# Opening of the first MLP: float32 squares and first copies on ScalarE, weights converted three steps after their load, one slice and one batch a step sooner

## The chip, the cores and the metric

The kernel runs on one core of a Trainium2 chip. The metric is the device time of one execution in microseconds (us), taken over several runs; lower is better. Times below are on the clock of one profiled execution, from the start of its span.

## What is computed

Attention over eight batches and eight heads with 32 learned packing queries, then two feed-forward blocks. Everything is float32; precision is kept by splitting each operand into a rounded high part and the rest, and multiplying three times (high x high, low x high, high x low).

```python
def sm_attn(qq, kk, vv):
    s = scale * np.matmul(qq, kk.transpose(0, 1, 3, 2))
    s = s - np.max(s, axis=-1, keepdims=True)
    a = np.exp(s)
    a = a / (np.sum(a, axis=-1, keepdims=True) + 1e-09)
    return np.matmul(a, vv)
p_packed = sm_attn(p, k, v)            # 8 x 8 x 32 x 64
out = sm_attn(q, p_packed, p_packed)   # 8 x 8 x 576 x 64
# x = out as 4608 tokens x 512
h = np.maximum(x @ w_in, 0.0)          # 512 x 2048
x = h * h @ w_out                      # 2048 x 512
# then a second MLP (512 x 1024 x 512) with SoLU and layer norm
```

## The kernel before, in words

The weights arrive as 64-bit floats. `Decode` (L105 to L133) loads one piece as pairs of 32-bit words (`raw`) and makes float32 of it (`dw`): ScalarE scales the high word (L122), VectorE shifts and merges bits (L123, L127, L129). Then ScalarE rounds the high part (`ws` for w_in, L271; `woh` for w_out, L320) and GpSimd takes the rest (L55).

The output projection of the attention is folded into the first weight matrix. `Unit.product` (L278) multiplies a unit, 256 rows by 256 columns of w_in, with the packed values `L` of four batches into PSUM (`pw`); ScalarE and VectorE copy it to `pws` as high and low part (L293, L294); and the sync queue (SP), which issues all transfers in program order, stores it at the head of the next step. Batch 0's columns of slices 0 and 1 go straight to `slot` in SBUF; all others go to `pw_d` in device memory and are read back by `load_slot` as needed. A slice is 256 of the 2048 hidden columns; there are eight. It is made from two units and serves two blocks of 128 columns, so four steps of a batch.

Then come the steps of the first MLP, listed in `steps`: each is (batch, half of its 576 tokens, block `fc` of 128 hidden columns). In step i, `h1` (L400) multiplies the attention weights of its batch (`ah`, `al`: high and low part) by the slot, and ScalarE takes the relu (`rg`, L413), GpSimd its float32 square (L414), ScalarE the rounded square (L415), VectorE the difference (L55). Four steps later `ymm` (L419) multiplies by w_out into the four PSUM tiles `Y`. Batches 0 and 1 go first and in turns: steps 0 to 3 use slice 0 of batch 0, 4 to 7 its slice 1, 8 to 15 both slices of batch 1, 16 and 17 slice 2 of batch 0, 18 and 19 its slice 3. Because Y is summed over a few blocks at a time there, it is copied out (L439 on ScalarE, L441 on VectorE) and later added to (L437). The first copies come at steps 5, 7, 15 and 19.

`clock` counts the steps of the outer loop (from L811): ten for the attention of the first packing, then T0 = 10 is step 0. `at_step` (L458) puts a load at a step; `unit_at` (L469) and `wout_at` (L481) put the three parts of a conversion k, k and k+1 steps behind it. `s2_jobs` (L329) lists the parts of one score slice of a batch: matmuls `s` against the packed keys `slc`, transposes, softmax, and the split into ah and al. PSUM tiles of `pw`, `h` and `s` share four banks.

Matmuls on TensorE, the sync queue and a few copies keep program order (`keep_in_program_order`, the calls through `pin`). All other instructions are put in order per engine by the tile framework, which simulates a timeline. At run time every engine runs its list in order: an instruction that waits holds up what is behind it.

Of the kernel before, what the change touches and what calls it, by code (L numbers as in the profile page):

```python
# [15 lines left out]
AF = mybir.ActivationFunctionType  # L16
ALU = mybir.AluOpType
# [18 lines left out]
def build(tc, qT, kT, vP, pT, w_in, w_out, w_in2, w_out2, g_ln, out):  # L36
    nc = tc.nc

    TURN = {n: cycle(x) for n, x in {"ETC": "VVA", "LNA": "AAAV"}.items()}
    V, A, G, PE, SP = nc.vector, nc.scalar, nc.gpsimd, nc.tensor, nc.sync  # L40


# [2 lines left out]
    def mm(*a, **k):  # L45
        pin(PE.matmul(*a, **k))  # L46

    def flip(own, *a):
        (pin if own else lambda x: x)(PE.transpose(*a))
# [94 lines left out]
    class Pack:  # L144
# [71 lines left out]
        def transp(self, n):  # L216
            t = self.pl.tile([P, KC * P], F32, tag="eT", name="eT", bufs=2) if self.own else t25("2", "eT")
            self.eT[n] = t.rearrange("p (k c) -> p k c", k=KC)
            for a, b in ((0, 3), (3, KC)):
                pt = bank("pt")[:, :(b - a) * P]  # L220
                for c in range(a, b):
                    flip(self.own, pt[:, (c - a) * P:(c - a + 1) * P], self.e1[n % 2][:, c * P:(c + 1) * P], ident)
                if next(TURN["ETC"]) == "A":
                    A.copy(t[:, a * P:b * P], pt)
# [33 lines left out]
    T0 = 10  # L258
    ring, clock = [0], [0]
# [140 lines left out]
    def h1(n):  # L400
        b, half, fc = n
        c = slice(half * HF, (half + 1) * HF)
        pb = bank("h1")
        w = slot[b, fc // 2][:, :, fc % 2]
        i = 0
        for g in range(2):
            ah, al = at[b, g]
            for l, x in ((0, ah), (1, ah), (0, al)):
                mm(pb[:, :HF], w[:, g, l], x[:, c], start=(i == 0), stop=(i == 5))
                i += 1  # L410
        rg, g2 = t25("1", "rg"), t25("2", "ghl", F32R)
        r, gg, gh, gl = rg[:, :HF], rg[:, HF:S], g2[:, :HF], g2[:, HF:S]
        A.activation(r, pb[:, :HF], AF.Relu)  # L413
        G.tensor_tensor(out=gg, in0=r, in1=r, op=ALU.mult)  # L414
        A.activation(gh, r, AF.Square)  # L415
        split_lo(V, gl, gg, gh)
        gt[n] = (gh, gl)

    def ymm(n):  # L419
        b, half, fc = n  # L420
        gh, gl = gt.pop(n)
        wh, wl = wo[fc]
        firsts = cuts.get(b, whole)
        for oc in range(4):
            o = slice(oc * P, (oc + 1) * P)
            for i, (w, x) in enumerate(((wh, gh), (wl, gh), (wh, gl))):
                mm(Y[oc], w[:, o], x, start=(fc in firsts and i == 0), stop=(fc + 1 in firsts and i == 2))
        if fc + 1 in firsts:
            c0 = b * S + half * HF
            new = (b, half) not in yp  # L430
            if new:
                yp[b, half] = ypp.tile([P, 4 * HF], F32, name=f"yp{half}") if b == 1 else sums()
            t = yp[b, half]
            for oc in range(4):
                o = t[:, oc * HF:(oc + 1) * HF]
                if not new:
                    V.tensor_tensor(out=o, in0=Y[oc], in1=o, op=ALU.add)  # L437
                elif oc % 2 == 0:
                    A.copy(o, Y[oc])  # L439
                else:  # L440
                    V.tensor_copy(o, Y[oc])  # L441
            if fc == 15:
                later.append(lambda: dma(y_d[:, :, c0:c0 + HF], t.rearrange("p (o c) -> p o c", o=4)))
# [25 lines left out]
    def unit_at(i, bg, s, g, pl, bufs):  # L469
        d = {}  # L470

        def begin():
            d["u"] = Unit(bg, s, g, pl(), bufs)
            queue.append(d["u"])

        at_step("first" if i == -5 else i, begin)
        k = 3 if i < -5 else 4
        for j in (k, k, k + 1):
            at_step(i + j, lambda: d["u"].d.step())

    def wout_at(i, fc):  # L481
        d = {}
        at_step("first" if i == -5 else i, lambda: d.setdefault("u", wout_unit(fc, win)))
        if i == -5:
            i = -4 + fc
        k = 3 if i < 0 else 4
        for j in (k, k, k + 1):
            at_step(i + j, lambda: d["u"].step())

    for b in range(2, B):  # L490
# [9 lines left out]
        for s in range(8):  # L500
            i = 16 + 2 * s + 3
            if b == 2:
                i = (17, 19, 21, 23, 25, 31, 33, 35)[s]
            if b == 4:
                i = max(i, 9 + 4 * s)
            at_step(base + i, lambda b=b, s=s: load_slot(b, s))
    for s, (i, k) in enumerate(((None, 4), (None, 6), (12, 13), (15, 16), (25, 26), (29, 30), (39, 40), (43, 44))):
        if i:
            at_step(i, lambda s=s: load_slot(0, s))
        at_step(k, lambda s=s: load_slot(1, s))  # L510
# [109 lines left out]
    for n in range(8):  # L620
        i = P1 + 1 + PS * n
# [109 lines left out]
    def h2(m):  # L731
# [15 lines left out]
        for i, h in enumerate(t):  # L747
# [16 lines left out]
            G.tensor_tensor(out=rstd, in0=rstd, in1=mhalf, op=ALU.pow)  # L764
            if next(TURN["LNA"]) == "V":
                V.tensor_scalar(out=h, in0=h, scalar1=mv[:, 0:1], scalar2=rstd, op0=ALU.subtract, op1=ALU.mult)
# [27 lines left out]
    def products():  # L794
        while queue and queue[0].ready():
            queue.pop(0).product()

    ps1 = {}
    early = {}
# [11 lines left out]
    for t in range(max(max(j for j in jobs if j != "first"), T0 + N + LAG - 1) + 2):  # L811
        i = t - T0
        clock[0] = t
        for fn in later:
            fn()
        later.clear()
        for n in ((0,), (1,), (2,), (3,), (4, 5), (6, 7))[t] if t < 6 else ():
            K0.load_v(n)
        if t + 3 < H:
            K0.load_k(t + 3)  # L820
        if t + 1 < H:
            K0.scores(t + 1)
        if t == 3:
            load_q(0)
        if t == 5:
            load_q(1)
            for j in jobs.pop("first"):
                j()
        if t == H:
            ps0_st.close()  # L830
            ps1["p"], ps1["st"] = pool("ps1", space=PSUM)
            Y += [ps1["p"].tile([P, HF], F32, name=f"Y{o}") for o in range(4)]
        if 0 <= t - 1 < H:
            K0.transp(t - 1)
        if t + 1 < H:
            K0.soft(t + 1)
        if 0 <= t - 2 < H:
            K0.packed(t - 2)
        if t in (4, 6, 8, 9):
            K0.pairs(t // 2 - 2 if t < 9 else 3)  # L840
        if t <= 9:
            products()
        if t == 6:
            for j in s2_jobs(0, 0, q0[0]):
                j()
        if t == 9:
            early[0] = s2_jobs(0, 1, q0[1], 2)
            for j in early[0][:9]:
                j()
            open_b()  # L850
            early[1] = s2_jobs(1, 0), s2_jobs(1, 1)
            for x in early[1]:
                x.pop(0)()
            early[1] = early[1][0] + early[1][1]
        if 0 <= i < N:
            h1(steps[i])
        for j in jobs.get(t, ()):
            j()
        products()
        if i == 0:  # L860
            for j in early[0][9:]:
                j()
        if 2 <= i < 8:
            for j in early[1][3 * i - 6:3 * i - 3]:
                j()
        if 0 <= i - LAG < N:
            ymm(steps[i - LAG])
# [121 lines left out]
```

## Time and profile before

| | us |
|---|---|
| runs of before | 1253.58, 1257.25, 1254.42 |
| median | 1254.42 |
| profiled execution, its own time | 1250.78 |
| its span in the profile | 1249.0 |
| TensorE busy in the span | 1159.8 |
| VectorE, ScalarE, GpSimd busy | 874.9, 639.3, 610.7 |

In the rows below PE is TensorE's matmuls, PEld its weight loads, DVE VectorE, ACT ScalarE, POOL GpSimd, SP the sync engine. L46 is line 46 of the kernel; as a helper issues matmuls, they are told apart by their tiles (out<-in, the numbers of the buffers left out). The time in brackets behind a row is how long the engine was idle ahead of it and what ended that. A matmul of 288 columns shows as 0.44 us or 0.30 us according to the clock that was granted.

### The profile page before, as it was taken

The numbers are of one execution on the slowest core, as the hardware profiler recorded it, in microseconds if no ns is written. First come the engines' busy times: TensorE is split into PE (matmuls) and PEld (weight loads), VectorE is DVE, ScalarE is ACT, GpSimd is POOL, SyncE is SP. The second block draws the span as 40 slices with busy tenths as digits, with TensorE's granted clock in tenths as the row PEclk, the third lists the DMA queues.
The fourth block names the chain that finished last, engine by engine and source line by source line (L and its number), as shares of the span: only waits on it lengthen the run. The fifth ranks groups of instructions, "written<-read, shape, count | busy, mean of one in ns | idle before, by whom it ended". The sixth has DMA issues, their size and how long they took to land.

```text
span 1249.0 us, 23478 instructions
## 1 busy us (share of the span) xinstructions
PE 1159.8 (93%) x8556; PEld 1064.5 (85%) x8556; DVE 874.9 (70%) x1722; ACT 639.3 (51%) x1413; POOL 610.7 (49%) x652
## 2 busy tenths in 40 slices
PE   6777699999999989999999999999999899998998
PEld 3456698898999878999999999998888788887888
DVE  4777588755436776575657733449898889989886
ACT  3444455444445554454555544346665556665554
POOL 1055355533324454443434433126886877886853
PEclk9768799999999998999999999999999999999999
DMA  9755777775144889556373482351112111111101
GB/s 329 228 169 141 230 218 231 259 253 189 59 171 148 250 249 305 161 177 250 139 281 134 157 334 104 124 168 35 34 40 64 34 39 63 35 39 42 56 27 43
DMA packets 97540, 187.66 MB, mean 150 GB/s; under 512 B 13968, under 2 KB 41616, under 8 KB 97424
## 3 DMA queue, kind: packets, MB, share of 16 engines
q1 hardware_dynamic: 97424, 186.16, 45.3%
q8 instruction: 67, 1.10, 0.4%
q14 instruction: 49, 0.40, 0.1%
HBM read 119.02 MB, written 66.06 MB: 148 GB/s over the span
## 4 chain that ended last, share of the span: by engine, by line
PE 60%; DVE 13%; POOL 10%; issue 6%; DMA 6%; ACT 4%; SPq 1%; ACTq 0%; DVEq 0%; POOLq 0%
PE Y L46 29%; PE h L46 13%; PE o L712 6%; PE h L712 5%; POOL y L682 3%; POOL cl L892 3%; PE s L46 3%; DMA yf<-y_d 2%; PE pw L46 2%; POOL rstd L764 1%; DVE dw L127 1%; POOL yf L675 1%; DMA raw<-w_out 1%; DVE dw L129 1%; DMA raw<-w_in 1%
## 5 line engine op out<-in xcount | busy, mean ns | idle before, releaser
L46 PE MATMUL Y<-ghl,woh 128*128 128x288 f32 x2048 | 469.4, 305 | 6.2 <-DVE yp L437 4.6
L46 PEld LDWEIGHTS Y<-ghl,woh 128*128 128x128 f32 x2048 | 349.9, 192 | 22.1 <-issue 8.5
L414 POOL TENSOR_TENSOR rg<-rg 128x288 f32<-128x288 f32 x256 | 188.3, 736 | 355.6 <-ACT rg L413 349.2
L46 PE MATMUL Y<-ghl,wol 128*128 128x288 f32 x1024 | 306.7, 300 | 0.0
L55 DVE TENSOR_TENSOR ghl<-rg,ghl 128x288 fp32r<-128x288 f32 x256 | 144.3, 567 | 201.8 <-ACT ghl L415 190.7
L46 PE MATMUL h<-ah,slot 128*128 128x288 f32 x1024 | 219.4, 303 | 24.3 <-ACT ah L388 9.2
L415 ACT ACTIVATE ghl<-rg 128x288 fp32r<-128x288 f32 x256 | 113.8, 445 | 189.3 <-PE Y L46 187.3
L712 PE MATMUL o<-wx,ch 128*128 128x256 f32 x1008 | 192.8, 288 | 8.7 <-ACT ch L891 4.7
L46 PEld LDWEIGHTS Y<-ghl,wol 128*128 128x128 f32 x1024 | 197.0, 192 | 0.0
L46 PEld LDWEIGHTS h<-ah,slot 128*128 128x128 f32 x1024 | 170.8, 195 | 27.6 <-issue 16.1
L712 PEld LDWEIGHTS o<-wx,ch 128*128 128x128 f32 x1008 | 162.5, 194 | 19.8 <-DVE ys L729 7.1
L46 PE MATMUL h<-al,slot 128*128 128x288 f32 x512 | 154.2, 301 | 0.9 <-POOL al L55 0.9
L712 PE MATMUL o<-wx,cl 128*128 128x256 f32 x504 | 143.3, 288 | 3.8 <-POOL cl L892 3.8
L892 POOL TENSOR_TENSOR cl<-raw,ch 128x512 fp32r<-128x512 f32 x84 | 120.3, 1439 | 41.1 <-ACT ch L891 40.9
L413 ACT ACTIVATE rg<-h 128x288 f32<-128x288 f32 x256 | 104.2, 407 | 55.3 <-PE h L46 46.9
L682 POOL TENSOR_TENSOR y<-yf,y 128x256 fp32r<-128x256 f32 x111 | 97.2, 887 | 31.1 <-ACT y L679 29.0
L712 PEld LDWEIGHTS o<-wx,cl 128*128 128x128 f32 x504 | 96.9, 194 | 6.6 <-POOL cl L892 5.3
L46 PEld LDWEIGHTS h<-al,slot 128*128 128x128 f32 x512 | 99.4, 194 | 1.2 <-POOL al L55 1.2
L891 ACT CAST ch<-raw 128x512 fp32r<-128x512 f32 x126 | 76.0, 620 | 39.2 <-DVE raw L897 25.2
L712 PE MATMUL h<-wi,y 128*128 128x512 f32 x312 | 84.2, 404 | 2.0 <-DVE hs L729 1.9
L679 ACT CAST y<-yf 128x256 fp32r<-128x256 f32 x120 | 47.0, 406 | 58.2 <-DVE yf L675 28.5
L55 POOL TENSOR_TENSOR ws<-dw,ws 128x512 fp32r<-128x512 f32 x32 | 41.9, 1312 | 70.4 <-ACT ws L271 70.4
(148 smaller groups left out, 1873.5 us busy)
## 6 DMA issues: line engine op xcount, KB each, us to landing
pw_d<-pws SPq DMA_DIRECT2D x124, 256.0 KB, 4.5
slot<-pw_d SPq DMA_DIRECT2D x62, 512.0 KB, 6.0
raw<-w_in SPq DMA_DIRECT2D x40, 512.0 KB, 6.2
raw<-w_out SPq DMA_DIRECT2D x24, 512.0 KB, 6.4
kf<-kT SPq DMA_DIRECT2D x32, 288.0 KB, 5.1
yf<-y_d SPq DMA_DIRECT2D x36, 256.0 KB, 3.0
out<-ys SPq DMA_DIRECT2D x72, 128.0 KB, 1.7
vf<-vP SPq DMA_DIRECT2D x16, 512.0 KB, 7.0
```

The lines of the kernel that those rows point to most:

```text
L46: pin(PE.matmul(*a, **k))
L55: eng.tensor_tensor(out=lo, in0=x, in1=f(hi), op=ALU.subtract)
L127: V.scalar_tensor_tensor(out=x, in0=self.hi, scalar=0x80000000, in1=x, op0=ALU.bitwise_and, op1=ALU.bitwise_or)
L129: V.scalar_tensor_tensor(out=x, in0=self.lo, scalar=29, in1=x, op0=ALU.logical_shift_right, op1=ALU.bitwise_or)
L413: A.activation(r, pb[:, :HF], AF.Relu)
L414: G.tensor_tensor(out=gg, in0=r, in1=r, op=ALU.mult)
L415: A.activation(gh, r, AF.Square)
L679: i = A.copy(c[n][0], x)
L682: (V if YS[cnt[1] % len(YS)] == 'V' else G).tensor_tensor(out=c[n][1], in0=x, in1=f(c[n][0]), op=ALU.subtract)
L712: PE.matmul(bk, x, w[:, y], start=(i == 0), stop=(i == 3 * nk - 1))
L891: A.copy(c[n][0], x)
L892: eng.tensor_tensor(out=c[n][1], in0=x, in1=f(c[n][0]), op=ALU.subtract)
```

## The change

In the first 20 steps the float32 square moves from GpSimd to ScalarE, and ScalarE makes all four first copies of Y instead of two. Units and pieces of w_out that are loaded before step 14 are converted three steps behind their load instead of four; the units of slice 1, loaded ahead of step 0, are then finished before step 0, and their products come two steps sooner. At the last step before step 0 the score matmuls of batch 0's second half go ahead of the product of the unit that is ready. Slice 2 is read back one step sooner for batches 0 and 1. The score jobs of batch 1 run four a step in steps 1 to 5 instead of three a step in steps 2 to 7. Copies of the transposed weights (`ETC`) alternate between VectorE and ScalarE, instead of two and one.

```diff
--- before.py
+++ after.py
@@ -36,7 +36,7 @@
 def build(tc, qT, kT, vP, pT, w_in, w_out, w_in2, w_out2, g_ln, out):
     nc = tc.nc
 
-    TURN = {n: cycle(x) for n, x in {"ETC": "VVA", "LNA": "AAAV"}.items()}
+    TURN = {n: cycle(x) for n, x in {"ETC": "VA", "LNA": "AAAV"}.items()}
     V, A, G, PE, SP = nc.vector, nc.scalar, nc.gpsimd, nc.tensor, nc.sync
 
 
@@ -411,7 +411,10 @@
         rg, g2 = t25("1", "rg"), t25("2", "ghl", F32R)
         r, gg, gh, gl = rg[:, :HF], rg[:, HF:S], g2[:, :HF], g2[:, HF:S]
         A.activation(r, pb[:, :HF], AF.Relu)
-        G.tensor_tensor(out=gg, in0=r, in1=r, op=ALU.mult)
+        if clock[0] < T0 + 20:
+            A.activation(gg, r, AF.Square)
+        else:
+            G.tensor_tensor(out=gg, in0=r, in1=r, op=ALU.mult)
         A.activation(gh, r, AF.Square)
         split_lo(V, gl, gg, gh)
         gt[n] = (gh, gl)
@@ -435,7 +438,7 @@
                 o = t[:, oc * HF:(oc + 1) * HF]
                 if not new:
                     V.tensor_tensor(out=o, in0=Y[oc], in1=o, op=ALU.add)
-                elif oc % 2 == 0:
+                elif oc % 2 == 0 or clock[0] < T0 + 20:
                     A.copy(o, Y[oc])
                 else:
                     V.tensor_copy(o, Y[oc])
@@ -474,7 +477,7 @@
             queue.append(d["u"])
 
         at_step("first" if i == -5 else i, begin)
-        k = 3 if i < -5 else 4
+        k = 3 if i < 14 else 4
         for j in (k, k, k + 1):
             at_step(i + j, lambda: d["u"].d.step())
 
@@ -483,7 +486,7 @@
         at_step("first" if i == -5 else i, lambda: d.setdefault("u", wout_unit(fc, win)))
         if i == -5:
             i = -4 + fc
-        k = 3 if i < 0 else 4
+        k = 3 if i < 14 else 4
         for j in (k, k, k + 1):
             at_step(i + j, lambda: d["u"].step())
 
@@ -504,7 +507,7 @@
             if b == 4:
                 i = max(i, 9 + 4 * s)
             at_step(base + i, lambda b=b, s=s: load_slot(b, s))
-    for s, (i, k) in enumerate(((None, 4), (None, 6), (12, 13), (15, 16), (25, 26), (29, 30), (39, 40), (43, 44))):
+    for s, (i, k) in enumerate(((None, 4), (None, 6), (11, 12), (15, 16), (25, 26), (29, 30), (39, 40), (43, 44))):
         if i:
             at_step(i, lambda s=s: load_slot(0, s))
         at_step(k, lambda s=s: load_slot(1, s))
@@ -838,14 +841,17 @@
             K0.packed(t - 2)
         if t in (4, 6, 8, 9):
             K0.pairs(t // 2 - 2 if t < 9 else 3)
-        if t <= 9:
+        if t < 9:
             products()
         if t == 6:
             for j in s2_jobs(0, 0, q0[0]):
                 j()
         if t == 9:
             early[0] = s2_jobs(0, 1, q0[1], 2)
-            for j in early[0][:9]:
+            for j in early[0][:2]:
+                j()
+            products()
+            for j in early[0][2:9]:
                 j()
             open_b()
             early[1] = s2_jobs(1, 0), s2_jobs(1, 1)
@@ -860,8 +866,8 @@
         if i == 0:
             for j in early[0][9:]:
                 j()
-        if 2 <= i < 8:
-            for j in early[1][3 * i - 6:3 * i - 3]:
+        if 1 <= i < 6:
+            for j in early[1][4 * i - 4:4 * i]:
                 j()
         if 0 <= i - LAG < N:
             ymm(steps[i - LAG])
```

How the instructions move, at three places. First TensorE around the products of slice 1 (`pw`, 12 matmuls a unit; `h` is a step, `s` a score slice of batch 1). Before, from step 1 on:

```order
L46 MATMUL h_790<-ah,slot 128x288 x2
L46 MATMUL h_790<-al,slot 128x288
L46 MATMUL h_790<-ah,slot 128x288 x2
L46 MATMUL h_790<-al,slot 128x288
L46 MATMUL h_809<-ah,slot 128x288 x2
L46 MATMUL h_809<-al,slot 128x288
L46 MATMUL h_809<-ah,slot 128x288 x2
L46 MATMUL h_809<-al,slot 128x288
L46 MATMUL pw<-ws,L 128x256 x24
L46 MATMUL s_869<-qf,slc 64x288 x2
L46 MATMUL s_870<-qf,slc 64x288 x2
```

Now, from the product of slice 0 that stood ahead of the scores of step 0:

```order
L46 MATMUL pw<-ws,L 128x256 x12
L46 MATMUL h_758<-ah,slot 128x288 x2
L46 MATMUL h_758<-al,slot 128x288
L46 MATMUL h_758<-ah,slot 128x288 x2
L46 MATMUL h_758<-al,slot 128x288
L46 MATMUL pw<-ws,L 128x256 x24
L46 MATMUL h_843<-ah,slot 128x288 x2
L46 MATMUL h_843<-al,slot 128x288
L46 MATMUL h_843<-ah,slot 128x288 x2
L46 MATMUL h_843<-al,slot 128x288
L46 MATMUL s_866<-qf,slc 64x288 x2
L46 MATMUL s_867<-qf,slc 64x288 x2
```

The 24 matmuls of slice 1 stand behind step 0 (h_758) instead of behind step 2 (h_809), and the scores of batch 1 behind step 1 instead of step 2.

Second, the sync queue after the first stores of slice 0 (`slot<-pws` and `pw_d<-pws` store a unit, `raw` loads weights, `slot<-pw_d` reads a slice back):

```order
-L52 DMA raw<-w_out 128x1024
-L52 DMA raw<-w_in 128x2x512
-L52 DMA raw<-w_out 128x1024
-L52 DMA slot<-pws 32x512 x4
-L52 DMA pw_d<-pws 32x4x512 x3
-L52 DMA slot<-pws 32x512 x4
-L52 DMA pw_d<-pws 32x4x512 x3
+L52 DMA slot<-pws 32x512 x4
+L52 DMA pw_d<-pws 32x4x512 x3
+L52 DMA slot<-pws 32x512 x4
+L52 DMA pw_d<-pws 32x4x512 x3
+L52 DMA raw<-w_out 128x1024
+L52 DMA raw<-w_in 128x2x512
+L52 DMA raw<-w_out 128x1024
```

The stores of slice 1's two units are now ahead of three weight loads that stood before them.

Third, ScalarE around the copies of slice 3's two products (`pws`), before:

```order
L320 CAST woh4_1323<-dw_1289 128x512
L122 ACTIVATE dw_1327<-raw_1138 128x512
L293 CAST pws_1346<-pw_1332 128x2x2x128
L293 CAST pws_1346<-pw_1333 128x2x2x128
L415 ACTIVATE ghl_1375<-rg_1374 128x288
L413 ACTIVATE rg_1428<-h1_1421 128x288
L439 COPY yp0_1453<-Y0_600 128x288
L439 COPY yp0_1453<-Y2_602 128x288
L320 CAST woh5_1382<-dw_1327 128x512
L293 CAST pws_1400<-pw_1386 128x2x2x128
L293 CAST pws_1400<-pw_1387 128x2x2x128
```

And now:

```order
L320 CAST woh4_1296<-dw_1258 128x512
L122 ACTIVATE dw_1300<-raw_1166 128x512
L293 CAST pws_1321<-pw_1307 128x2x2x128
L293 CAST pws_1321<-pw_1308 128x2x2x128
L418 ACTIVATE ghl_1350<-rg_1349 128x288
L413 ACTIVATE rg_1401<-h1_1394 128x288
L415 ACTIVATE rg_1401<-rg_1401 128x288
L320 CAST woh5_1355<-dw_1300 128x512
L293 CAST pws_1373<-pw_1359 128x2x2x128
L293 CAST pws_1373<-pw_1360 128x2x2x128
```

The second product's copies (pws_1373) stand ahead of the copies of Y; the relu between is that of step 14 (rg_1401) instead of step 15, and the new float32 square follows it (L415, in place on rg).

## Rows read from the trace of the kernel before

**Rows 1.** Head of the profile page.
```profile
span 1249.0 us, 23478 instructions
```
**Rows 2.** Stretches: length; busy (count) of PE, PEld, DVE, ACT, POOL; clock; DMA share; GB/s.
```profile
60.00:80.00 20.00, 12.59 (x56) 9.00 (x55) 17.81 (x28) 10.42 (x22) 10.92 (x10) 0.50 0.51 147
80.00:102.00 22.00, 14.53 (x83) 13.19 (x84) 15.53 (x25) 10.29 (x23) 12.20 (x13) 0.81 0.53 161
102.00:148.00 46.00, 34.67 (x225) 32.02 (x225) 31.37 (x50) 20.04 (x44) 19.18 (x19) 0.83 0.73 200
148.00:260.00 112.00, 107.35 (x786) 101.65 (x787) 83.34 (x149) 57.37 (x131) 52.45 (x58) 0.96 0.72 234
```
**Rows 3.** Waits of TensorE from 50 to 260 us: total us, times, longest.
```profile
PE h L46 <- ACT ah L388: 9.2, 2, 5.1
PE h L46 <- DMA slot<-pws: 6.2, 2, 4.3
PE h L46 <- DMA slot<-pw_d: 6.1, 1, 6.1
...
PE h L46 <- DVE pws L294: 2.8, 1, 2.8
```
**Rows 4.** Timeline of TensorE: start, us, what, times, idle before.
```profile
59.58 0.85 PE L46 MATMUL h<-ah,slot 128*128 128x288 f32 x2 [4.04 <-ACT ah L388]
...
68.47 1.22 PE L46 MATMUL pw<-ws,L 64*128 64x256 f32 x8 [0.56 <-POOL ws L55]
...
81.47 0.82 PE L46 MATMUL h<-ah,slot 128*128 128x288 f32 x2 [4.33 <-DMA slot<-pws]
...
86.52 1.19 PE L46 MATMUL s<-qf,slc 128*64 128x288 f32 x8
...
102.00 0.44 PE L46 MATMUL Y<-ghl,woh 128*128 128x288 f32 x1
```
**Rows 5.** Groups by line, 59 to 148 us: busy us, mean ns, idle before.
```profile
L414 POOL TENSOR_TENSOR rg<-rg 128x288 f32<-128x288 f32 x18 | 14.8, 822 | 46.4 <-ACT rg L413 46.4
...
L122 ACT ACTIVATE dw<-raw 128x512 f32<-128x512 f32 x14 | 9.2, 664 | 1.2 <-POOL wol L55 1.0 <-POOL ws L55 0.2
...
L415 ACT ACTIVATE ghl<-rg 128x288 fp32r<-128x288 f32 x18 | 8.0, 444 | 10.6 <-PE Y L46 10.3
...
L439 ACT COPY ys<-Y 128x288 f32<-128x288 f32 x4 | 1.6, 396 | 1.6 <-PE Y L46 1.6
```
**Rows 6.** Timeline of ScalarE, 114 to 138 us.
```profile
114.38 0.65 ACT L122 ACTIVATE dw<-raw 128x512 f32<-128x512 f32 x1
...
123.84 0.62 ACT L271 CAST ws<-dw 128x512 fp32r<-128x512 f32 x1 [2.63 <-DVE dw L129]
...
128.29 0.62 ACT L320 CAST woh<-dw 128x512 fp32r<-128x512 f32 x1 [2.64 <-DVE dw L129]
...
129.38 1.06 ACT L293 CAST pws<-pw 128x512 fp32r<-128x512 f32 x2
...
136.08 1.07 ACT L293 CAST pws<-pw 128x512 fp32r<-128x512 f32 x2
```
**Rows 7.** Timeline of the sync queue, 71 to 80 us.
```profile
71.56 0.34 SPq L52 DMA_DIRECT2D raw<-w_out  x1
72.00 2.42 SPq L52 DMA_DIRECT2D slot<-pws  x4
...
76.42 3.50 SPq L52 DMA_DIRECT2D slot<-pws  x4
```
**Rows 8.** Chain of waits ahead of step 18: start, us, what.
```profile
138.01 3.66 DMA pw_d<-pws
141.69 5.72 DMA slot<-pw_d
```
**Rows 9.** Timeline of VectorE, 64 to 67 us.
```profile
64.06 1.52 DVE L55 TENSOR_TENSOR ghl<-rg,ghl 128x288 fp32r<-128x288 f32 x1
...
66.11 0.44 DVE L55 TENSOR_TENSOR ghl<-rg,ghl 128x288 fp32r<-128x288 f32 x1
```

## The prediction

> **What bounds the kernel now.** I read the time of the profiled execution first: its span is 1249.0 us [rows 1] and its own time 1250.78 us, 3.6 us under the median of 1254.42. Then the table of stretches: from 148 to 260 us TensorE is busy for 107.35 of 112 us, while between 60 and 148 us it is busy for 61.8 of 88 and its granted clock is 0.50, 0.81 and 0.83 [rows 2]. So the change, nearly all of which lies before the end of step 19, is worth what it takes out of that early stretch. What arrives at 148 us sooner arrives at the end sooner, since all that follows is laid out by step numbers. Third, TensorE's waits: for the rounded attention weights (ah) 9.2 us in two waits, for the weight slice (slot) stored from pws 6.2, for a slice read back from pw_d 6.1, for the copies out of PSUM (pws) 2.8 [rows 3]. They lie at step 0, which begins at 59.58 after 4.04 us; at step 4, whose second half begins at 81.47 after 4.33 [rows 4]; at step 8 (the longer wait for ah, 5.1), step 15 (pws) and step 18 (the read-back) [rows 3].
>
> **The change, part by part.** Everything is placed on the clock of the profiled execution.
>
> *Prices.* A square on ScalarE takes 0.444 us, a copy of Y there 0.396; on GpSimd a square took 0.822 [rows 5]. So 20 squares and 8 copies put 20 x 0.444 + 8 x 0.396 = 12.1 us more on ScalarE in about 90 us, in which it is busy for 10.4 of 20, 10.3 of 22 and 20.0 of 46 [rows 2]. As a share that fits; where ScalarE stands in front of a wait I count it there.
>
> *At nothing:* the copies of the transposed weights, of which ScalarE gets three more and VectorE three fewer before step 0 (TensorE waits there for other things; if the cover is gone, 3 x 0.4); the w_out conversions and the slices for steps 16 and 24, for which TensorE has no wait now [rows 3] and which come sooner still.
>
> *Step 0: 0.0.* The score matmuls of the second half go ahead of a product of 12 matmuls, about 1.7 us by the row of eight in 1.22 [rows 4]. Against it the two units of the second slice are now converted earlier, and on VectorE their bit operations stand ahead of the last split of the packed values, for which the same scores wait. I take the two as equal. Bounds: 1.7 us gained; 2.8 lost, if a whole conversion of 4.46 us [rows 6] stood in the way.
>
> *Step 4: -4.5.* The second half of the slice arrived at 81.47. Its product ended at 69.7 (68.47 + 1.22) [rows 4], but its store was issued only at 76.42: the sync queue first waited to issue a weight load at 71.56, then issued the first group of stores from 72.00 on [rows 7]. In the changed order both products stand right behind step 0, and the weight loads come after the stores. Step 0 ends at about 60.7, the first product at 62.4. The second needs the PSUM bank of step 0, which ScalarE empties at about 63.8, since a rounding of w_out and a first conversion operation stand ahead there; it ends at 65.4. With copies out of PSUM as long as now, the first group can be stored at 67.5. The queue takes 4.4 us from there to the second (72.00 to 76.42) and 5.05 more to its arrival (76.42 to 81.47): 77.0 in place of 81.47. Bounds: 0, and -6.2, both waits gone [rows 3].
>
> *Scores of batch 1: -1.1.* The second set of 1.19 us at 86.52 [rows 4] moves ahead of step 4, where TensorE would wait anyway. Bounds 0 and -1.2.
>
> *Step 8: -1.2.* This wait is for the last attention weights of batch 1, and here the added work on ScalarE lies in front of it. From the first copy of Y, at about 82.2 in the changed kernel, ScalarE has in order: 8 copies, 3 float32 and 3 rounded squares, 2 relus, 3 first conversion operations (0.664 [rows 5]), 2 roundings of weights and 4 of attention weights, 11.4 us, and is through at 93.6; with the split on GpSimd behind it, step 8 ends at about 95.2. Now it ends at 102.0 [rows 4]. Of the 6.8 us between, 5.6 are the two terms above. The four weight loads that wait behind the stores are issued at about 77; a transfer of that size took 5.72 [rows 8], so they are there at 83 to 85, just as ScalarE comes to their conversions. Bounds: -5.1, the wait gone; +4, if these loads come that much later and hold up the copies of Y behind them.
>
> *Step 18: -7.6.* The slice used there is stored, then read back: 3.66 and 5.72 us [rows 8], which stay. What sets their start is a chain of conversions. ScalarE begins the first unit at 114.38, rounds one at 123.84 and the next at 128.29, so 4.45 us a link, and copies the last product at 136.08 [rows 6]. The chain now begins one step sooner, some 4.5 us. Its three links lose perhaps 0.4 each, since no square on GpSimd holds up VectorE: a split took 1.52 us beside GpSimd and 0.44 alone [rows 9]. The last product's copies, now 6.7 us behind the ones before (129.38 to 136.08) because a relu and two copies of Y that wait for TensorE stand between, come in the new order ahead of the copies of Y, in about 4.8. Sum 4.5 + 1.2 + 1.9 = 7.6; the slice arrives at about 133.1, and TensorE, which has work of its own until about 130.7, still waits. Bounds: 0, and -10, TensorE's own work.
>
> The Trainium skill ("SBUF — State Buffer", "SBUF: two separate sides") states that VectorE and GpSimd share one pair of ports, which the one that starts first holds for its whole instruction. By that rule alone 18 squares of 0.822 could give VectorE back up to 14.8 us, and the sum would be some 13 us lower than by the 1.2 that I count from the rows; the trace agrees with the hold-up, 1.52 against 0.44, but TensorE mostly waits for others.
>
> *Sum.* 0.0 - 4.5 - 1.1 - 1.2 - 7.6 = -14.4. The placing assumes that every instruction starts as soon as its inputs are there. I take back 2.4, about two hold-ups like 1.52 against 0.44 [rows 9]: -12.0, so 1238.8 against the profiled 1250.78, and **1242.4** against the median.
>
> **The rivals.** About 0.3% (3.8 us) is what a measurement can tell from no change.
>
> *Only the store order pays.* Step 18 gains nothing, because ScalarE, with another 0.444 a step, keeps the links at 4.45, and the chain's sooner start is eaten at step 8. For it: ScalarE stands in every link. Against it: it idles 2.6 us in each, waiting for VectorE [rows 6]. Then -4.5 - 1.1 = -5.6: 1248.8.
>
> *The clock comes back sooner.* Matmuls are packed more closely from step 1 to 8, and the granted clock, 0.50 from 60 to 80 [rows 2], which is the lower level of 1.2 GHz, rises to 2.4 GHz two steps earlier than now; their matmuls take half, about 4 us: 1238. Against it: gaps at steps 4 and 8 remain in my own placing. The Trainium skill ("TensorE: Matmul & The Clock Gate", "HAM oscillation — how this bites in real kernels") has it that each such gap throttles the array anew; by that rule my sum, which leaves gaps at steps 4, 8, 14 and 18, keeps the low clock as now.
>
> *The waits only move.* The loads and the read-back set the time, and what TensorE gains before step 18 it waits there: 1253.
>
> *Slower: ScalarE becomes the bound.* It runs in order. If the relu of a step falls behind the float32 square of the one before, the copies of Y and the conversions, the step waits for ScalarE. This decides from where ScalarE's work in a step passes TensorE's, some 2.4 us at full clock: a relu and two squares are 1.3, a unit's two operations 1.3, four copies 1.6. Only steps with copies and a conversion pass it. Were it so throughout, all 12.1 us would land on the path, less the 4.5 of step 4: +7.6, 1262. Against it: those steps are four of the 20, and four PSUM banks lie between.
>
> **How the numbers follow.** My forecast 0.50, the store order alone 0.17, the clock 0.14, waits moved 0.09, slower 0.10. Faster by over 0.3%: 0.50 + 0.17 + 0.14 = 0.81; within 0.3%: 0.09; slower: 0.10. The range goes from 1236, where step 18 is at its bound of -10 and the clock helps too, to 1255, and leaves out the slower rival and a little below.
>
> **What would show it.** In the changed profile the wait for the stored slice should be one, near 77 us; step 8 should end near 95 and step 18 start between 133 and 137 (now 147.4, where the read-back ends [rows 8]); GpSimd should have no square before step 20; ScalarE should be busy for over 60% of the time between steps 4 and 8. I am wrong if step 18 starts when it does now in spite of fewer waits before it (waits moved), if TensorE waits for a relu in most steps (slower), or if the gain lies after step 19, where I see none.

## The result, and the profile after

The changed kernel took 1242.8 us (median of four runs, 1240.66 to 1245.53) against 1254.6: ratio 0.9904, 95% interval 0.9874 to 0.9933, so 11.8 us less by the medians and 0.96% by the ratio. 1242.4 had been forecast. Built once more beside other kernels it gave 1242.78 us, ratio 0.9927 (0.9908 to 0.9947). Its profiled execution took 1240.66 us.

Two lines of the page of the changed kernel, below them the second of these of the kernel before, and the table of stretches of the changed kernel (length; busy time and count of PE, PEld, DVE, ACT and POOL; granted clock; DMA share; GB/s):

```profile
span 1238.6 us, 23434 instructions
...
PE 1148.9 (93%) x8556; PEld 1054.8 (85%) x8556; DVE 868.3 (70%) x1708; ACT 651.1 (53%) x1447; POOL 595.7 (48%) x632
```

```profile
PE 1159.8 (93%) x8556; PEld 1064.5 (85%) x8556; DVE 874.9 (70%) x1722; ACT 639.3 (51%) x1413; POOL 610.7 (49%) x652
```

```profile
60.00:80.00 20.00, 13.76 (x81) 11.15 (x82) 12.81 (x24) 10.27 (x23) 6.20 (x5) 0.76 0.66 157
80.00:102.00 22.00, 16.83 (x102) 14.85 (x101) 18.57 (x24) 15.72 (x38) 11.55 (x9) 0.77 0.57 208
102.00:148.00 46.00, 37.12 (x264) 35.28 (x261) 27.17 (x49) 26.90 (x63) 10.30 (x9) 0.89 0.79 229
148.00:260.00 112.00, 106.99 (x808) 100.11 (x808) 88.91 (x165) 59.04 (x136) 56.83 (x63) 1.00 0.76 245
76.00:94.00 18.00, 13.11 (x75) 12.04 (x75) 12.33 (x17) 12.32 (x31) 8.36 (x8) 0.80 0.82 274
```

From 60 to 148 us TensorE is now busy for 67.7 us instead of 61.8 [rows 2]. ScalarE, between steps 4 and 8 (last row), is busy for 12.32 of 18 us, 68%.

TensorE's five longest waits in the changed kernel between 50 and 260 us, on its timeline (start, us, what, times, idle before):

```profile
61.34 0.82 PE L46 MATMUL h<-ah,slot 128*128 128x288 f32 x2 [7.03 <-DMA slot<-pws]
...
76.23 0.65 PE L46 MATMUL h<-ah,slot 128*128 128x288 f32 x2 [4.43 <-DMA slot<-pws]
...
92.14 0.85 PE L46 MATMUL h<-ah,slot 128*128 128x288 f32 x2 [2.90 <-ACT ah L388]
...
119.20 0.51 PE L46 MATMUL h<-ah,slot 128*128 128x288 f32 x2 [2.33 <-DVE pws L294]
...
135.29 0.82 PE L46 MATMUL h<-ah,slot 128*128 128x288 f32 x2 [6.23 <-DMA slot<-pw_d]
```

These rows stand against [rows 3, 4]. The wait for ah at step 0 has gone, and one for slot has taken its place; the second half of step 4 begins at 76.23 instead of 81.47; step 8 ends at 94.30 instead of 102.21; step 18 begins at 135.29 instead of 147.55, 12.26 us sooner. At the end of the span 10.4 of them are left (1249.0 less 1238.6).

### The profile page after: what moved, and what is told of

Read it like the earlier page. It is cut to its first block, busy times and chain, and to the rows that moved or that the text cites. A ratio compares the mean times of both kernels' runs of the same rounds, so it can differ in the third digit from the quotient of the medians.

```text
span 1238.6 us, 23434 instructions
## 1 busy us (share of the span) xinstructions
PE 1148.9 (93%) x8556; PEld 1054.8 (85%) x8556; DVE 868.3 (70%) x1708; ACT 651.1 (53%) x1447; POOL 595.7 (48%) x632
## 4 chain that ended last, share of the span: by engine, by line
PE 51%; DVE 17%; POOL 12%; issue 8%; DMA 6%; ACT 4%; SPq 1%; ACTq 0%; DVEq 0%; POOLq 0%
PE Y L46 28%; PE h L46 13%; POOL y L685 4%; POOL cl L898 3%; DMA yf<-y_d 3%; PE o L715 3%; PE s L46 3%; PE h L715 2%; DVE hs L759 2%; PE pw L46 1%; POOL rstd L767 1%; POOL yf L678 1%; DVE st L762 1%; DVE dw L127 1%; DMA pw_d<-pws 1%
## 5 line engine op out<-in xcount | busy, mean ns | idle before, releaser
L417 POOL TENSOR_TENSOR rg<-rg 128x288 f32<-128x288 f32 x236 | 173.0, 734 | 312.9 <-ACT rg L413 310.4
L46 PE MATMUL h<-ah,slot 128*128 128x288 f32 x1024 | 215.7, 299 | 24.4 <-DMA slot<-pws 11.5
L46 PEld LDWEIGHTS h<-ah,slot 128*128 128x128 f32 x1024 | 167.3, 191 | 27.0 <-issue 14.9
```

## The experiments

Twelve runs followed, eleven of other kernels and one of the changed kernel again. Four places tell them apart, all read on TensorE's timeline: the start of the second half of steps 0 and 4, the end of step 8, the start of step 18. They come from one profiled execution each; the ratio comes from 4 to 12 runs, against the kernel before on the same chip.

| kernel | step 0 | step 4 | end of 8 | step 18 | ratio (95%) |
|---|---|---|---|---|---|
| before | 59.58 | 81.47 | 102.21 | 147.55 | |
| changed | 61.34 | 76.23 | 94.30 | 135.29 | 0.9904 (0.9874 to 0.9933) |
| changed, again | 61.49 | 76.45 | 94.38 | 135.11 | 0.9927 (0.9908 to 0.9947) |
| squares and copies alone | 60.23 | 80.57 | 100.50 | 145.29 | 0.9972 (0.9956 to 0.9988) |
| conversions alone | 62.50 | 76.57 | 99.48 | 142.07 | 0.9978 (0.9962 to 0.9993) |
| score jobs alone | 60.11 | 82.04 | 93.79 | 142.78 | 0.9966 (0.9953 to 0.9978) |
| conversions and score jobs | 64.42 | 78.55 | 95.88 | 140.99 | 0.9944 (0.9927 to 0.9961) |
| all but the conversions | 60.94 | 81.94 | 93.74 | 139.11 | 0.9924 (0.9902 to 0.9947) |
| all but the squares | 62.23 | 77.90 | 97.15 | 138.16 | 0.9898 (0.9876 to 0.9920) |
| all but the score jobs | 62.01 | 76.97 | 95.80 | 137.14 | 0.9923 (0.9909 to 0.9937) |
| product first | 62.84 | 76.93 | 93.04 | 137.10 | 0.9917 (0.9903 to 0.9932) |
| w_out at 12, 13, 15, 17 | 61.23 | 76.10 | 94.37 | 132.22 | 0.9944 (0.9930 to 0.9959) |
| w_out at 12, 13, 13, 13 | 61.48 | 76.50 | 95.40 | 136.74 | 0.9928 (0.9910 to 0.9946) |
| the same, squares back | 60.19 | 75.82 | 94.91 | 135.19 | 0.9946 (0.9926 to 0.9966) |

An interval is some 1.5 to 4 us wide on either side, so a difference of two rows under 3 us is not settled by its ratio.

### Single parts on the kernel before

Squares and copies alone:

```diff
-        G.tensor_tensor(out=gg, in0=r, in1=r, op=ALU.mult)
+        if clock[0] < T0 + 20:
+            A.activation(gg, r, AF.Square)
+        else:
+            G.tensor_tensor(out=gg, in0=r, in1=r, op=ALU.mult)
...
-                elif oc % 2 == 0:
+                elif oc % 2 == 0 or clock[0] < T0 + 20:
```

> The kernel before with only the squares and the copies of Y of the first 20 steps moved to ScalarE; every load, conversion, product and step stays where it was. Theory (the timetable pays: conversions, products and stores begin sooner): the waits for slot at step 4 (81.47 us) and at step 18 (147.55) depend on conversions that begin at the same step, so step 4 moves by under 0.5 us, step 18 by 1 to 2, and the time by -2 to +1 us. Rival (the ports pay: no square on GpSimd holds up VectorE): most of the gain is here, -6 to -12 us, with VectorE's split (L55) near 0.45 us everywhere in the first 20 steps.

It gained 3.5 us by the medians (1251.04 against 1254.51): more than the theory's bound of 2, less than the rival's 6 at the least. Step 4 moved by 0.9 and step 18 by 2.26. VectorE's groups between 59 and 148 us (busy us, mean ns), first of the kernel before, then of this one:

```profile
L127 DVE SCALAR_TENSOR_TENSOR dw<-raw,dw 128x512 uint32<-128x512 uint32 x14 | 13.2, 946 | 0.2
L55 DVE TENSOR_TENSOR ghl<-rg,ghl 128x288 fp32r<-128x288 f32 x18 | 12.5, 696 | 10.3 <-ACT ghl L415 10.0
L129 DVE SCALAR_TENSOR_TENSOR dw<-raw,dw 128x512 uint32<-128x512 uint32 x14 | 11.2, 802 | 0.2
L123 DVE TENSOR_SCALAR dw<-dw 128x512 uint32<-128x512 uint32 x14 | 9.6, 685 | 5.2 <-ACT dw L122 5.0
```

```profile
L129 DVE SCALAR_TENSOR_TENSOR dw<-raw,dw 128x512 uint32<-128x512 uint32 x14 | 12.0, 858 | 0.2
L123 DVE TENSOR_SCALAR dw<-dw 128x512 uint32<-128x512 uint32 x14 | 10.8, 769 | 5.3 <-ACT dw L122 5.0
L127 DVE SCALAR_TENSOR_TENSOR dw<-raw,dw 128x512 uint32<-128x512 uint32 x14 | 10.5, 748 | 0.2
L55 DVE TENSOR_TENSOR ghl<-rg,ghl 128x288 fp32r<-128x288 f32 x18 | 10.1, 562 | 10.9 <-ACT ghl L418 10.7
```

The same 60 instructions took VectorE 46.5 us before and 43.4 now. Moving the squares gave it back 3.1 us, not the 14.8 that they had lasted on GpSimd: the split and L127 became shorter, the two other bit operations longer. One reason is that it was not a square that stood beside the split of 1.52 us at 64.06 [rows 9]. GpSimd's row there is the rest of a weight, which stays where it was:

```profile
63.86 1.40 POOL L55 TENSOR_TENSOR ws<-dw,ws 128x512 fp32r<-128x512 f32 x1 [0.27 <-ACT ws L271]
```

In the kernel before, nine of the 18 splits have nothing on GpSimd beside them and take some 0.45 us; none that has only a square beside it takes over 0.92.

Conversions alone:

```diff
-        k = 3 if i < -5 else 4
+        k = 3 if i < 14 else 4
...
-        k = 3 if i < 0 else 4
+        k = 3 if i < 14 else 4
```

> The kernel before with only the conversions of units and of w_out loaded before step 14 put three steps behind their load instead of four. Theory (timetable): most of the gain is here: step 4 sooner by some 4 us, because the products and their stores come two steps sooner; step 18 sooner by 4.5 more from the chain of units; in all -6 to -10 us. Rival (ports): the conversions only crowd VectorE and GpSimd more, and the waits move: -3 to +2 us.

It gained 2.8 us by the ratio (4.0 by the medians), so the theory's "most of the gain" is wrong; by the ratio the rival's range holds. TensorE's waits from 50 to 150 us show why:

```profile
PE h L46 <- ACT ah L388: 16.3, 2, 8.2
...
PE h L46 <- DMA slot<-pws: 4.9, 1, 4.9
```

Step 4 does come 4.9 us sooner, as placed. But step 0 comes 2.9 us later, because the conversions of slice 1 now lie among the softmax of its scores, and at step 8 TensorE waits for ah for 8.19 us instead of 5.13: what step 4 gains is waited for there.

Score jobs alone:

```diff
-        if 2 <= i < 8:
-            for j in early[1][3 * i - 6:3 * i - 3]:
+        if 1 <= i < 6:
+            for j in early[1][4 * i - 4:4 * i]:
```

> The kernel before with only the score jobs of batch 1 moved: four a step in steps 1 to 5 instead of three in steps 2 to 7. Reading A (the sum of the prediction): this is worth the 1.1 us of its own scores and a part of the 1.2 at step 8, so -1 to -2 us, and step 12 (114.17 us in the kernel before) moves by no more. Reading B (from the run without the earlier conversions, where step 4 stayed and step 8 had no wait for ah): this is the part that takes out the wait of step 8; step 12 comes 5 to 7 us sooner, step 4's wait for slot stays near 4.3, and the time is 4 to 7 us lower.

Reading B held up to step 8: the wait for ah there is gone, and step 8 ends 8.4 us sooner although step 4 is no sooner (82.04). But the time fell by 4.0 us, the least that it allows, and step 12 came not 5 to 7 but 3.7 us sooner (it begins at 116.17 in the kernel before, where 114.17 was written by mistake, and at 112.44 here). Rows of TensorE's timeline behind step 8 say what is late instead:

```profile
94.63 0.40 PE L46 MATMUL Y<-ghl,wol 128*128 128x288 f32 x1 [0.66 <-POOL wol L55]
...
101.23 0.40 PE L46 MATMUL Y<-ghl,woh 128*128 128x288 f32 x1 [1.53 <-ACT woh L320]
102.56 0.61 PE L46 MATMUL Y<-ghl,wol 128*128 128x288 f32 x1 [0.94 <-POOL wol L55]
```

TensorE now overtakes the conversions, which still come four steps behind their load.

Conversions and score jobs together (both edits above):

> The kernel before with two parts of the change only: conversions three steps behind the load, and the score jobs of batch 1 four a step from step 1. Reading B (the two belong together: the earlier slice is only worth something if the attention weights of batch 1 are there at step 8): nearly the whole gain, -8 to -11 us, more than the sum of each alone (-2.8 and -4.3). Reading A (each part pays its own terms): -5.5 to -7.5 us, the sum of the two alone, and the squares on ScalarE make up the rest.

7.1 us, the sum of the two alone, as reading A has it. The interval goes from 4.9 to 9.1 us, so the low end of reading B is not excluded. The whole change gained 9.1 us by the ratio of the same batch and 12.0 by that of its first runs, so some 2 to 5 us come from the rest.

### Single parts taken out of the changed kernel

The conversions back to four steps:

```diff
-        k = 3 if i < 14 else 4
+        k = 3 if i < -5 else 4
...
-        k = 3 if i < 14 else 4
+        k = 3 if i < 0 else 4
```

> The changed kernel with the conversions four steps behind the load again (as before), all else of the change in. Theory (timetable): most of the gain is lost: step 4 near 81 us, step 18 near 145, time 1248 to 1254. Rival (ports): the gain stays, 1241 to 1246.

Step 4 is back at 81.94, as expected, and yet the time is 1245.71: 8.8 us of the gain stay. Step 8 ends at 93.74, as in the changed kernel. What the conversions add lies behind it, at step 18 (139.11 against 135.29), and is some 3 us of the time by the medians; the ratios (0.9924 against 0.9904 and 0.9927) do not settle it. The time lies in the rival's range, but the ports are not shown as the cause: step 8 ends early with the score jobs alone, too (93.79).

The squares back on GpSimd, the copies left on ScalarE:

```diff
-        if clock[0] < T0 + 20:
-            A.activation(gg, r, AF.Square)
-        else:
-            G.tensor_tensor(out=gg, in0=r, in1=r, op=ALU.mult)
+        G.tensor_tensor(out=gg, in0=r, in1=r, op=ALU.mult)
```

> The changed kernel with the 20 float32 squares on GpSimd again; ScalarE keeps the four copies of Y. Theory (timetable): step 4 (76.23 us) is the same within 0.5; step 18 (135.29) is later by 0 to 2, as a split takes up to 1.5 us instead of 0.45 beside a square; time +0 to +2 us over the changed kernel. Rival (ports): +6 us or more. Third reading (ScalarE is nearly the bound in steps 8 to 14): the time falls by 1 to 2 us as copies out of PSUM (pws) no longer queue behind squares.

1241.79 us, no slower than the changed kernel. Step 4 (1.7 later) and step 18 (2.9 later) moved by more than the theory allows, but its profiled execution is its slowest (1245.9), so the later places in the table say little. The move that names the change is worth nothing that this run can tell, once the rest is there; another pair of runs, below, leans the other way.

The score jobs back to three a step from step 2 (the third edit above, reversed):

> The changed kernel with the score jobs of batch 1 as before, three a step in steps 2 to 7. Reading A: +1 to +2.3 us over the changed kernel (1242.8). Reading B: what step 4 gains is waited for again at step 8 (a wait for ah of 6 to 8 us there), step 12 is at 110 to 112 instead of 106.94, and the time is +3 to +5 us, 1246 to 1248.

1243.31 us, 0.5 over the changed kernel, and a ratio that does not tell them apart. Step 8 waits 4.51 us for ah, not 6 to 8, and ends 1.5 us later. At that place this is reading A, near the 1.1 of the prediction. Step 12 begins at 110.17, which seems to be reading B's number, but the base it started from was misread: the changed kernel begins step 12 at 108.68 (106.94 lies inside step 11). So step 12, too, is 1.5 later.

The product ahead of the scores again, at the last step before step 0:

```diff
-        if t < 9:
+        if t <= 9:
             products()
...
-            for j in early[0][:2]:
-                j()
-            products()
-            for j in early[0][2:9]:
+            for j in early[0][:9]:
                 j()
```

> The changed kernel with the product of slice 0's second unit ahead of the score matmuls again, at the last step before step 0. Theory: the wait of 7.03 us for slot at step 0 comes from this swap, since the copies of that product (pws) now stand behind VectorE's softmax of the scores and its store is issued at 57.3 instead of 53.8 us; with the product first the store is issued near 54, the second half of step 0 waits for ah alone and starts at 59.5 to 60.5 instead of 61.34, and the time is 0.5 to 1.5 us lower. Rival: the earlier conversions of slice 1 crowd VectorE there and hold up the attention weights instead, so that step 0 starts at 61.5 or later and the time is 0 to +1.5.

The theory is half right. The sync queue does issue the store early again; its timeline, of the changed kernel and of this one:

```profile
57.30 2.45 SPq L52 DMA_DIRECT2D slot<-pws  x4
```

```profile
53.44 2.41 SPq L52 DMA_DIRECT2D slot<-pws  x4
```

But TensorE's row at step 0 is now this, later than with the swap:

```profile
62.84 0.85 PE L46 MATMUL h<-ah,slot 128*128 128x288 f32 x2 [7.62 <-ACT ah L388]
```

The rival is right. With conversions at three steps and the product first, step 0 starts at 62.50, 62.84 and 64.42 (three kernels); with the scores first it starts between 60.19 and 62.23 (seven executions of six kernels). The swap pays back a part of what the earlier conversions cost there. The time, 1243.03, does not move.

### Ahead of step 18

On ScalarE's timeline of the changed kernel, and in the chain of waits that ends at step 18 (start, us, what):

```profile
116.21 0.62 ACT L320 CAST woh<-dw 128x512 fp32r<-128x512 f32 x1 [1.72 <-DVE dw L129]
116.74 0.66 ACT L122 ACTIVATE dw<-raw 128x512 f32<-128x512 f32 x1
117.30 1.06 ACT L293 CAST pws<-pw 128x512 fp32r<-128x512 f32 x2
...
121.79 1.07 ACT L293 CAST pws<-pw 128x512 fp32r<-128x512 f32 x2
```

```profile
112.07 4.64 DMA raw<-w_out
...
128.37 6.78 DMA slot<-pw_d
...
135.29 1.78 PE h L46 x6
```

Slice 3's first product ended at 110.94 and is copied from 117.30 on, behind the rounding of one piece of w_out (L320) and the first conversion of another (L122), whose load landed at 116.7; neither is used before step 20. It is not the load that holds the copies, though. In the changed kernel run again they begin at 117.39 all the same, and no load of w_out is in the chain; what they stand behind is the rounding, which waits 1.72 us for VectorE's last operation of that conversion (L129). The four loads, and with them the conversions, were moved:

```diff
-    for fc, i in enumerate((-5, -5, 1, 2, 8, 9, 11, 12, 21, 23, 24, 26, 36, 38, 40, 42)):
+    for fc, i in enumerate((-5, -5, 1, 2, 12, 13, 15, 17, 21, 23, 24, 26, 36, 38, 40, 42)):
```

> The changed kernel with the four pieces of w_out for steps 16 to 19 loaded at steps 12, 13, 15 and 17 instead of 8, 9, 11 and 12, which is early enough for TensorE (first used at step 20). Theory: ahead of step 18 the copies of slice 3's products (pws) stand on ScalarE behind conversions of w_out that wait for their load (a product that ended at 110.94 us is copied at 117.30); without them the copies follow their products, the wait for pws at step 14 (2.33) goes, the read-back is issued 3 to 5 us sooner, step 18 starts at 130 to 132 instead of 135.29, time -3 to -5 us. Rival: the stores and the read-back on the sync queue set step 18 anyway, or the moved conversions are late at step 20: -1 to +2.

Step 18 began at 132.22, 3.1 us sooner. The first product's copies now begin on ScalarE at 113.21 instead of 117.30, the last one's at 119.32 instead of 121.79, and this is the chain:

```profile
114.49 1.29 DVE pws L294 x2
...
116.16 3.77 DMA pw_d<-pws
119.93 1.29 DVE pws L294 x2
...
125.69 6.40 DMA slot<-pw_d
...
132.22 1.02 PE h L46 x6
```

That the conversions of w_out held up these copies is shown, then; but the time was 1246.34, 3.5 over the changed kernel, where the rival allowed 2. Its second half came true, some steps later. At steps 22 and 23 the matmuls of Y wait for the late pieces:

```profile
145.20 0.40 PE L46 MATMUL Y<-ghl,wol 128*128 128x288 f32 x1 [1.12 <-POOL wol L55]
...
151.53 0.61 PE L46 MATMUL Y<-ghl,woh 128*128 128x288 f32 x1 [1.75 <-ACT woh L320]
```

Two versions between, with 12, 13, 13, 13 in that list, and with the squares back on GpSimd besides:

> The changed kernel with the four pieces of w_out for steps 16 to 19 loaded at steps 12, 13, 13 and 13 (before: 8, 9, 11, 12; in the run with 12, 13, 15, 17 step 18 started at 132.22 us but TensorE then waited for woh and wol at steps 22 and 23). Theory: step 18 starts at 131 to 133 as there, the waits for woh and wol behind it do not come back, and the gain of 3 us stays: 1238 to 1241. Rival: four conversions together hold up the relus of steps 18 to 20 on ScalarE, or the loads the read-back: 1242 to 1246.

> As the run before it (w_out loaded at 12, 13, 13, 13), with the 20 float32 squares on GpSimd again. If the squares on ScalarE are worth nothing in the presence of the rest, as the run with the squares back says (ratio 0.9898 against 0.9904), the time is within 1.5 us of the run before it; if ScalarE's freed time shortens the conversions crowded around step 18, 1 to 3 us lower; if GpSimd's squares hold up VectorE there, 1 to 3 us higher.

Neither gained: 1243.73 and 1245.78 us beside 1242.78 of the changed kernel in the same batch. The second is 2.05 us above the first, as the last of its three readings has it (GpSimd's squares hold up VectorE, 1 to 3 us), but the two intervals overlap. With the 1.0 us by which the other kernel with the squares back lies below the changed one, their price in the whole is open, between -1 and +2. In the first, step 18 did not come sooner at all (136.74). Its last copies begin on ScalarE at 120.98 (119.32 in the run before), and its chain shows what followed:

```profile
121.56 1.11 SPq L52
...
122.71 1.09 SPq L52
...
123.85 0.44 SPq L52
...
124.39 6.89 DMA pw_d<-pws
...
131.30 5.30 DMA slot<-pw_d
```

The sync queue issues the three weight loads of step 13 first, so the store goes out at 124.39; it then takes 6.89 us, beside those loads (the first product's store took 3.77 in the run before), and the read-back has to wait for it. The rival's second half was right.

No version beat the changed kernel by more than the intervals.

Its repetition, as the base of that batch:

> The changed kernel again, unaltered, beside the three others of this batch, as their base. Every theory: 1241 to 1245 us, ratio to the kernel before 0.990 within 0.003.

## Why the prediction was right, and where its steps were not

The sum, -14.4 less a haircut of 2.4, was to bring step 18 forward by 12.0; it came 12.26 sooner, and the time followed. The ratio excludes three of the rivals (only the store order, the waits only move, ScalarE the bound); the clock's 1238 lies just outside. The signs that were named held, but for one: the waits for the stored slice are two, not one. That step 18 fell so close is in part luck: an error of 2.0 us there and the haircut, which was meant for something else, cancel. And what comes sooner at step 18 does not simply come sooner at the end: the rest of the span took 1101.5 us in the kernel before, 1103.3 in the changed one, and up to 1109.7 (w_out at 12, 13, 15, 17). Step by step:

- **Step 0, 0.0: it cost 1.8** (61.34 against 59.58), inside the bounds. I had weighed 1.7 us for the scores against conversions on VectorE, and missed what stands behind the swapped product: its copies wait behind the softmax, and its store was issued at 57.30 instead of 53.77. The wait for ah became one for slot.
- **Step 4, -4.5: -5.2.** The stores went ahead of the weight loads as the order had it, and the slice arrived at 76.2, where 77.0 was forecast. The step that failed is what I made of it: I booked this as a gain of the whole. Alone it is worth 2.8 us, and without it 8.8 remain. Step 8 goes by the attention weights of batch 1 more than by step 4: it ends at 99.48 with the conversions alone, at 93.79 with the score jobs alone.
- **Batch 1's scores and step 8, -1.1 and -1.2: -2.7 together** (7.91 less 5.24). On top of the rest they are worth what was booked (1.5 at step 8 when they are put back). Alone they bring step 8 forward by 8.4, as much as everything together. So the gains at steps 4 and 8 do not add at step 8, and my terms were right only in this order.
- **Step 18, -7.6: -4.4** (12.26 less 7.91). Up to the last product's copies the sum held without its haircut: they begin at 121.79 instead of 136.08 [rows 6], 14.29 us sooner, where 14.4 was forecast (the terms up to step 8 gave 1.1 more than booked, the chain 1.2 less), and 4.5 behind the ones before, where I had 4.8. The term that failed is the store and the read-back, "which stay". From these copies to step 18 it is 13.50 us instead of 11.47. The sync queue issues the eight stores of both units in one row and then a weight load, and the read-back takes 6.78 us instead of 5.72 [rows 8]:

```profile
120.29 7.29 SPq L52 DMA_DIRECT2D pw_d<-pws  x8
127.62 0.66 SPq L52 DMA_DIRECT2D raw<-w_in  x1
128.37 1.67 SPq L52 DMA_DIRECT2D slot<-pw_d  x2
```

The haircut of 2.4 was meant for hold-ups on VectorE; that it is near these 2.0 is luck. The conversions of w_out ahead of the copies are no error of the sum but a gain left lying, 3.1 us at step 18.
- **The squares.** 0.444 us was forecast for one on ScalarE, 0.454 is the mean there, and ScalarE did not become the bound. The links of the chain lost the 0.4 us forecast: ScalarE's roundings at 108.10, 112.17 and 116.21 are 4.07 and 4.04 us apart, instead of 4.45, and with the squares back on GpSimd 4.70 and 4.45 (110.73, 115.43, 119.88). But VectorE as a whole did not gain much: 3.1 us of its busy time with the squares alone. The 1.52 us that I gave to a square beside the split belonged to another instruction, as shown above. The Trainium skill ("SBUF — State Buffer", "SBUF: two separate sides") speaks of an exclusive lock on the shared ports; by that rule alone up to 14.8 us could have come back. The trace agrees that a single instruction of VectorE can be longer beside one of GpSimd's (1.52 us against 0.45), not that each square costs VectorE its length.
- **The clock.** It did come back sooner: 0.76 instead of 0.50 of full speed from 60 to 80 us. It paid nothing there, because the matmuls that became faster were followed by 4.43 us of waiting for slot, which hangs on copies and transfers. Over the whole span it shows more than my sum allowed for. At a mean granted clock of 0.978 instead of 0.966 TensorE's 8556 matmuls took 10.9 us less busy time than before, and its idle time (span less busy) did not fall: 89.7 us against 89.2. Ahead of step 18 the same matmuls took 8.4 us less and the idle time fell by 3.8; in the changed kernel run again it is 5.0 and 7.4. So the sum was right about when the slices arrive, but the waits for them became hardly shorter: what shrank is largely TensorE's work between them. Whether TensorE would have been ready as early at the old clock is not shown, so this rival is not cleared away.

What stays open is how the gain divides. The squares with the copies, the conversions and the score jobs gain 0.28, 0.22 and 0.34% alone, 0.84% together, near the 0.73 and 0.96% of the whole; yet none of the three (the squares without the copies) costs more than the intervals when it is taken out. The smaller parts (the copies, the swap, the slice read back earlier, the copies of the transposed weights) lie within the intervals as well, and no run took the copies, the slice or the transposed weights alone.

## What to carry to other kernels

Where waits follow each other on one engine, a part's price is what it adds when the next wait is still there: ask of every stall removed which wait comes next and what ends that one. Here either of two edits could be taken out of the whole and step 8 came at most 1.5 us later, though alone they brought 2.7 and 8.4; and parts worth 3 to 4 us each alone cost -1 to 3 when taken out. A transfer's time does not stay when what is queued around it moves: ask what its queue will hold at the new time. An in-order engine delays a copy behind a conversion that nobody needs yet; moving the conversion helps only if its load does not then stand in the queue, or in time, ahead of something else.

## What had not been expected of the hardware

The same two short waits are followed by different clocks. At about 405 us, far behind the change, TensorE waits 0.92 and 1.27 us in the kernel before, and 0.92 and 1.26 in the one with the squares alone. First the kernel before, its timeline of TensorE and the stretch of 10 us around it, then the other:

```profile
406.54 0.47 PE L46 MATMUL pw<-ws,L 64*128 64x256 f32 x3 [0.92 <-DVE pws L294]
408.28 0.74 PE L46 MATMUL pw<-ws,L 64*128 64x256 f32 x8 [1.27 <-POOL ws L55]
```

```profile
400.00:410.00 10.00, 7.74 (x60) 6.92 (x57) 8.74 (x12) 5.53 (x14) 7.28 (x8) 1.00 0.88 225
```

```profile
404.40 0.47 PE L46 MATMUL pw<-ws,L 64*128 64x256 f32 x3 [0.92 <-DVE pws L294]
406.14 1.22 PE L46 MATMUL pw<-ws,L 64*128 64x256 f32 x8 [1.26 <-POOL ws L55]
```

```profile
400.00:410.00 10.00, 7.73 (x46) 6.90 (x45) 7.55 (x11) 5.15 (x12) 6.18 (x6) 0.77 0.90 227
...
410.00:420.00 10.00, 10.00 (x73) 9.70 (x72) 4.80 (x8) 4.65 (x11) 3.13 (x4) 0.89 0.74 222
```

In one the eight matmuls behind take 0.74 us, at the higher level of 2.4 GHz; in the other 1.22, at 1.2 GHz, and the clock is not back until after 410. The Trainium skill ("TensorE: Matmul & The Clock Gate", "HAM oscillation — how this bites in real kernels") has TensorE's wait for a transfer between groups of matmuls throttle the array every time; that is a longer wait than these. All 14 profiled executions have these two waits, of 0.92 or 0.93 and 1.26 or 1.27 us: in six the eight matmuls took 0.74 us, in eight 1.22 or 1.23. How much of the 8 us by which runs of one kernel differ comes from this is not shown. The profiled execution of the squares alone (1255.56 us) was the slowest of its twelve although it reached step 18 sooner than the kernel before, but the clock is the smaller part of that: behind step 18 it took 6.8 us longer than the kernel before, and of these TensorE was busy for 1.8 and idle for 5.0.
